# Heads' products of a fused attention and MLP kernel, two groups in a row in the first layer of batches 4 to 7

## The chip, the cores and the metric

The kernel runs on one core of a Trainium2 chip. The metric is the time of one execution on the device in microseconds (us). Engine names are those of the profile: PE (TensorE, matmuls), PEld (its weight loads), ACT (ScalarE), DVE (VectorE), POOL (GpSimd), SP (SyncE, which issues the DMAs).

## The reference

Eight batches, eight heads of 64, 576 tokens; then a layer norm and a two-layer MLP over the 512 columns that the heads make together, with a residual. All inputs are fp32.

```python
# attention, q k v: [8, 8, 576, 64], 32 landmarks = means over 18 tokens each
A = sm(q, k_lm);  Bm = sm(q_lm, k_lm);  C = sm(q_lm, k)      # softmax of scaled products
Z = Bm^T / (norm1(Bm) * norminf(Bm) + 1e-06)
for _ in range(6):
    Z = 2 * Z - Z @ Bm @ Z
x = A @ Z @ C @ v                                             # heads side by side: [8, 576, 512]
# MLP, w_ch1: [512, 2048], w_ch2: [2048, 512]
xn = (x - mean(x)) / sqrt(var(x) + 1e-06) * g_ln
out = x + relu(xn @ w_ch1) @ w_ch2
```

## The kernel before

**The algebra around the change.** The first layer isn't computed from `x`. With `ea` the exponentials of A (already divided by their sums) and `Z C v` small per head (32 landmarks by 64), the product `x @ W1` is taken as `ea^T (Z C v W1)`: per batch, the transposed small matrices `zt` are first multiplied with the (scaled and centred) weights `w1_16`. These are the *heads' products*. They come in four groups `f`, one for each 512 of the 2048 hidden columns. Each group is 8 matmuls with 64 rows and 32 columns of weights (`zt`) and 512 streamed columns, one on each of the eight 64x32 parts of PE's array; they fill two PSUM banks, one for each unit `u` of four heads. ACT or DVE then casts both banks to fp16 into the SBUF tile `m16[f]` (three buffers).

**Chunks.** A batch's hidden values are made in 16 chunks of 128 hidden columns (`chunk(m)`), four to each group: 4 matmuls of 288 columns into `psh`, a PSUM tile of two banks, then one eviction with the ReLU on ACT (or DVE) into `hT`. Chunk `m` reads `m16[m // 4]`. In the kernel before, group 0 is made before chunk 0, and groups 1, 2 and 3 after the chunks 0, 4 and 8: three chunks ahead of their first use.

**Second layer.** `hT` and `w2_16` are multiplied in blocks of 128 tokens, 16 matmuls of 512 columns each, for batches 0 to 3. From batch 4 on (`FAST`) the first four blocks go by `seven_products`, seven products of halves in place of eight, with 256 columns each, whose operands (`w2mix`, and sums within `hT`) POOL and DVE mix beforehand. DVE adds the result, scaled, to `x`, and SP stores it.

**x itself** is made by `rows_of`: matmuls of `ea` with `zcbd` (256 columns, two for each block of tokens), copied out of PSUM by ACT or DVE into `xblk`.

**PSUM.** Eight banks: four single ones (`banks`, L424) that heads' products, rows of `x`, attention's small products and the second layer's sums take in turn, and a ring `ps2` (L421) with two places of two banks each, tag "p2". Attention's scores and sums and every chunk take these places in turn, so a new tile waits until the tile before last has been read out.

**What sets the order of the work.** Every engine runs its instructions in the order in which the program issues them. The program is written by one loop (`run`, L1512) over four streams: attention of the coming batches, first layers, batch 0's rows, second layers. Each stream yields a function that says from when on its next step could run without waiting. The loop goes through the streams in that order and issues the next step of the first one that is ready by its own running estimate of all engines (`Clock`, L83); if none is, of the one that is ready soonest. So a wait in one stream is filled with steps of another, mostly second-layer matmuls, as long as there are any. `help_out` (L1427) issues loads, casts, statistics and mixing on the other engines in between. `sooner` (L518) gives a cast to ACT or DVE, whichever the estimate has free first, and `chunk` does the same for its eviction. Since all instructions go through helpers, nearly all matmuls have line L274 (`MM`) in the profile and nearly all other operations L268; the names of the tiles tell them apart.

The places that the change touches: `First.product_of_heads` (L1138) and `first_layer` (L1174).

Of the kernel before, what the change touches and what calls it, by code (L numbers as in the profile page):

```python
# [10 lines left out]
FP32 = mybir.dt.float32  # L11
# [5 lines left out]
P = 128  # L17
# [3 lines left out]
def kernel(  # L21
# [21 lines left out]
    U = H // 4  # L43
# [10 lines left out]
        name=nc.get_next_instruction_name(), act_func_set_id=6, ins=[], outs=[]))  # L54
# [163 lines left out]
    clock = Clock()  # L218
# [54 lines left out]
    def MM(o, l, r, rb=0, cb=0, start=True, stop=True, skip=False):  # L273
        keep(nc.tensor.matmul(o, l, r, start=start, stop=stop, tile_position=(rb, cb),  # L274
                              skip_group_check=(skip or cb != 0)))
# [75 lines left out]
    for i in range(NV):  # L351
        t = const.tile([P, U, NJ, 2, D + 1], FP16, name=f"natv{i}")
# [9 lines left out]
    for u in range(U):  # L362
        for nm in ("q", "k"):
            t = nat.tile([P, NJ, 2, D], FP16, name="nat", tag="nat")
# [16 lines left out]
    def less(f):  # L381
        return less_[f // 2][:, f % 2, :]
# [35 lines left out]
    mprod = Ring(name="mprod", bufs=3)  # L418
    mhT = ctx.enter_context(tc.tile_pool(name="mhT", bufs=1))

    ps2 = Ring(name="ps2", bufs=2, space=bass.MemoryType.PSUM)  # L421
# [42 lines left out]
    banks = Banks()  # L464
# [53 lines left out]
    def sooner(n, at=0.0):  # L518

        a = max(clock.free["Activation"], at) + 190 + 0.79 * n  # L520
        return scalar.copy if a <= max(clock.free["DVE"], at) + 140 + 1.15 * n else (
            lambda o, i: dve.tensor_copy(out=o, in_=i))
# [607 lines left out]
    class First:  # L1130
# [5 lines left out]
            self.m16 = {}  # L1136

        def product_of_heads(self, f):  # L1138
            self.m16[f] = mprod.tile([P, U, 512], FP16, name="m16", tag="m16")
            psm = [banks.take([P, 512]) for _ in range(U)]  # L1140
            for r in range(2):
                for e in range(2):
                    for u, (w, _) in enumerate(self.units):
                        rows, cb = ds(64 * e, 64), 32 * (2 * (e ^ u) + r)
                        MM(psm[u][ds(cb, 32), :], self.zt[rows, r, w, :],
                           w1_16[rows, 2 * u + r, ts(f, 512)], rb=64 * e, cb=cb, skip=True)
            if f in centered:
                for u in range(U):
                    sooner(512, clock.at(psm[u]))(self.m16[f][:, u, :], psm[u])
                return  # L1150
            n = 2 if (self.b, f) == (0, 0) else 1
            for part in range(n):
                cols = ts(part, 512 // n)
                for u, (_, total) in enumerate(self.units):
                    dve.scalar_tensor_tensor(
                        out=self.m16[f][:, u, cols], in0=less(f)[:, cols], scalar=total,
                        in1=psm[u][:, cols], op0=ALU.mult, op1=ALU.add)
            if self.b == LAST_WHOLE:
                whole.extend((f, c) for c in (0, 2))
# [14 lines left out]
    def first_layer(b):  # L1174
        l1 = First(b)
        if b == 0:
            yield from first_layer0(l1)
            return
        yield lambda: max(banks.next(2), mprod.next("m16"), clock.at(l1.zt))
        l1.product_of_heads(0)  # L1180
        for m in range(MCH):
            yield lambda: max(ps2.next("p2"), clock.at(l1.m16[m // 4], *l1.ea))
            l1.chunk(m)
            if m == 3:
                begun_first[0] = b
            if m % 4 == 0 and m < 12:
                yield lambda: max(banks.next(2), mprod.next("m16"))
                l1.product_of_heads(m // 4 + 1)
        for t in l1.ea:
            aexp.unpin(t)  # L1190
        if b in (0, 1, 2, 4, 6, 7):
            asm.unpin(l1.zt)
# [3 lines left out]
    def first_layer0(l1):  # L1196
        l1.product_of_heads(0)
        scale_w1(5, 1, scalar)
        for m in range(MCH):
            yield lambda: max(ps2.next("p2"), clock.at(l1.m16[m // 4], *l1.ea))  # L1200
            l1.chunk(m)
            chunks0[0] = m + 1
            if m == 0:
                scale_w1(7, 1, scalar)
            if m in (2, 6):
                f = 2 if m == 2 else 3
                for c in range(KCH):
                    yield lambda: max(0.0 if c else banks.next(), clock.at_key(w1_16[:, c, ts(f, 512)]))
                    if c == 0:
                        psf_of[f] = banks.hold([P, 512])  # L1210
                        mine = banks.last
                    MM(psf_of[f][:], lesser[:], w1_16[:, c, ts(f, 512)], start=(c == 0),
                       stop=(c == KCH - 1))
                scalar.copy(less(f), psf_of.pop(f)[:])
                banks.release(mine)
            if m in (1, 5, 9):
                yield lambda: max(banks.next(2), mprod.next("m16"))
                l1.product_of_heads(m // 4 + 1)
# [272 lines left out]
    def first_layers():  # L1491
        for b in range(B):
            yield lambda: 0.0 if b == 0 or (b in ready and current[0] == b - 1
                                            and (b <= LAST_WHOLE or len(centered) == 4)) else NEVER
            yield from first_layer(b)
            first_done.add(b)
            if b >= FAST:
                h_left.extend((b, i, k) for i in range(3) for k in (0, 4))
            if b == 0:
                keep_tail(0)  # L1500
# [109 lines left out]
```

## Time and profile before

| | |
|---|---|
| median of 3 runs | 282.48 us (282.12 to 282.77) |
| the profiled execution | 282.81 us |
| its span, first to last instruction | 281.0 us |
| PE busy | 266.2 us in 3618 matmuls |
| DVE, ACT, POOL busy | 212.3, 161.9, 160.1 us |
| heads' products `bank<-w,zt`, all batches | 256 matmuls in 32 groups |
| chunks `psh<-ea,m` | 512 matmuls, 286 ns each by the profile |
| chunk evictions on ACT, on DVE | 115 of 652 ns, 13 of 750 ns |
| casts into `m16` on ACT, on DVE | 30 of 588 ns, 18 of 679 ns |

Times are of one profiled execution. A row of the timeline has a start, the time from the first start to the last end, engine, line, operation, out<-in by tile names, shape and count, and in brackets the idle time before it and what ended it. A matmul's duration has its pipeline in it: consecutive matmuls overlap, so what a piece costs PE is read from the start of one piece to the start of the next. The page cuts the span into 40 slices of 7.0 us, and gives the busy share of each in tenths.

In the profiled execution the first layers of batches 5, 6 and 7 run from 183.0 to 197.1 us, 205.7 to 219.8 and 239.2 to 253.0, that of batch 4 from 145.8 to 160.5; the attention of batches 5 and 6 is spread from 146.7 to 179 us, that of batch 7 from 220.7 to 235 us, and the second layer fills the rest.

### The profile page before, as it was taken

How to read it: one execution, taken by the hardware profiler on the slowest of the kernel's cores; microseconds unless marked ns; L12 is line 12 of the kernel's file. 1: busy time of each engine (PE TensorE's matmuls, PEld its weight loads, DVE VectorE, ACT ScalarE, POOL GpSimd, SP SyncE). 2: the span in 40 equal slices, each digit the busy share in tenths (PEclk: the TensorE clock that was granted, in tenths of full speed). 3: DMA queues.
4: the chain of work that ended last, by engine and by line, in shares of the span. 5: the costliest groups of instructions: out<-in, count | busy, mean ns of one | idle time of the engine just before them, and what ended most of it. 6: DMA issues, size and time to landing. Idle time of an engine off the chain costs nothing.

```text
span 281.0 us, 8678 instructions
## 1 busy us (share of the span) xinstructions
PE 266.2 (95%) x3618; PEld 165.6 (59%) x3618; DVE 212.3 (76%) x479; ACT 161.9 (58%) x287; POOL 160.1 (57%) x187
## 2 busy tenths in 40 slices
PE   7988999999999999889989999999999999999994
PEld 7744554355444564344555645567877666678883
DVE  3558985999999847888978384697885499748761
ACT  2676954368554887148889754698248733671000
POOL 5368778999999999978999999310000040100000
PEclk9999999999999999999999999999999999999998
DMA  7999999989745579893750101310060005300606
GB/s 244 384 387 388 388 388 392 354 278 266 246 126 160 152 249 304 265 279 95 221 188 2 34 8 45 72 40 0 2 144 9 1 5 118 72 0 2 149 22 167
DMA packets 23375, 46.70 MB, mean 166 GB/s; under 512 B 2212, under 2 KB 2472, under 8 KB 23336
## 3 DMA queue, kind: packets, MB, share of 16 engines
q1 hardware_dynamic: 23176, 46.02, 51.9%
q8 instruction: 28, 0.46, 0.7%
q10 hardware_dynamic: 160, 0.13, 0.2%
q14 instruction: 11, 0.09, 0.1%
HBM read 36.70 MB, written 9.44 MB: 164 GB/s over the span
## 4 chain that ended last, share of the span: by engine, by line
PE 79%; DVE 9%; ACT 5%; issue 3%; DMA 2%; SPq 0%; DVEq 0%; ACTq 0%
PE bank L274 51%; PE psh L274 21%; DMA stg<-in_q_dram 2%; ACT hT L268 2%; DVE xblk L268 2%; PE pscv L274 2%; DVE m L268 2%; DVE xT L268 1%; PE psec L274 1%; PE psd L274 1%; DVE part L268 1%; ACT ec L268 1%; DVE hT L268 1%; ACT lns L268 1%; PE psea L274 1%
## 5 line engine op out<-in xcount | busy, mean ns | idle before, releaser
L274 PE MATMUL bank<-w,hT 128*128 128x512 f16 (+1 forms) x528 | 109.2, 335 | 1.1 <-issue 1.0
L268 ACT ACTIVATE hT<-psh 128x576 f16<-128x576 f32 x115 | 71.0, 652 | 17.4 <-PE psh L274 16.0
L274 PE MATMUL psh<-ea,m 128*128 128x288 f16 x512 | 76.9, 286 | 2.8 <-ACT hT L268 2.1
L274 PEld LDWEIGHTS <-hT 128*128 128x128 f16 x656 | 60.4, 98 | 32.2 <-issue 6.9
L274 PEld LDWEIGHTS <-m 128*128 128x128 f16 x512 | 47.9, 97 | 25.3 <-issue 10.1
L268 DVE SCALAR_TENSOR_TENSOR xblk<-bank,rstd,xblk 128x256 f32<-128x256 f32 (+1 forms) x77 | 39.2, 541 | 18.2 <-PE bank L274 18.2
L268 POOL TENSOR_TENSOR ea<-ea,lns 128x576 f16<-128x576 f16 x14 | 18.1, 1306 | 47.2 <-ACT lns L268 47.0
L268 POOL CAST nat<-stg 128x1152 f16<-128x1152 f32 x28 | 32.6, 1181 | 2.0 <-DMA stg<-in_k_dram 1.1
L268 POOL CAST natv<-stg 64x1152 f16<-64x1152 f32 (+1 forms) x23 | 26.7, 1161 | 8.8 <-DMA stg<-in_v_dram 7.9
L268 ACT COPY xblk<-bank 128x512 f32<-128x512 f32 (+1 forms) x34 | 19.1, 588 | 12.2 <-PE bank L274 12.0
L268 DVE BATCH_NORM_STATS2 six<-xblk 128x6 f32<-128x512 f32 x36 | 24.2, 671 | 0.0
L268 ACT CAST m<-bank 128x512 f16<-128x512 f32 x30 | 17.0, 588 | 9.9 <-PE bank L274 9.9
L268 DVE STREAM_TRANSPOSE xT<-nat 128x576 uint32<-128x576 uint32 x28 | 21.4, 765 | 0.6 <-POOL nat L268 0.6
L268 ACT ACTIVATE lns<-psd 128x576 f32<-128x576 f32 x16 | 10.3, 646 | 17.8 <-PE psd L274 16.7
L268 DVE TENSOR_REDUCE part<-xT 128x32 f16<-128x576 f16 x28 | 20.0, 742 | 0.2
L268 POOL TENSOR_TENSOR asum<-asum 128x256 f32<-128x256 f32 (+1 forms) x28 | 18.0, 644 | 2.2
L268 DVE CAST m<-bank 128x512 f16<-128x512 f32 x18 | 12.2, 679 | 7.3 <-PE bank L274 7.2
L268 POOL TENSOR_TENSOR asum<-nat 128x512 f32<-128x512 f16 x14 | 16.5, 1178 | 1.1
L274 PE MATMUL bank<-w2mix,hT 128*128 128x256 f16 x128 | 16.5, 273 | 0.0
L274 PE MATMUL bank<-w2mix 128*128 128x256 f16 x128 | 16.0, 273 | 0.0
L268 DVE SCALAR_TENSOR_TENSOR st<-st,bank 128x128 f16<-128x128 f16 (+2 forms) x36 | 11.1, 308 | 6.4 <-PE bank L274 6.0
L274 PE MATMUL bank<-zcbd,ea 128*128 128x256 f16 (+1 forms) x80 | 14.4, 275 | 1.0 <-DVE m L268 0.8
(123 smaller groups left out, 341.6 us busy)
## 6 DMA issues: line engine op xcount, KB each, us to landing
stg<-in_q_dram SPq DMA_DIRECT2D x16, 576.0 KB, 5.7
stg<-in_k_dram SPq DMA_DIRECT2D x16, 576.0 KB, 5.4
stg<-in_v_dram SPq DMA_DIRECT2D x16, 576.0 KB, 7.1
out_dram<-xblk SPq DMA_DIRECT2D x70, 128.0 KB, 2.3
wstg<-in_moe_w_ch_dram SPq DMA_DIRECT2D x16, 512.0 KB, 7.1
out_dram<-xblk ACTq DMA_DIRECT2D x2, 64.0 KB, 2.3
out_dram<-xblk SPq DMA_DIRECT2D x2, 64.0 KB, 2.1
g_rows<-in_moe_g_ln_dram SPq DMA_DIRECT2D x1, 2.0 KB
```

The costliest lines, as they stand in the source:

```text
L268: return lambda *args, **kw: keep(getattr(self.engine, op)(*args, **kw))
L274: keep(nc.tensor.matmul(o, l, r, start=start, stop=stop, tile_position=(rb, cb), skip_group_check=(skip or cb != 0)))
```

## The change

For batches 4 to 7, groups 0 and 1 are made together before chunk 0, and groups 2 and 3 together after chunk 4. The first group of each pair takes two of the four single banks as before; the second takes a tile of the ring, one of the two places that the chunks use. All 16 matmuls are issued in a row, then the four casts, first group first. The step waits for two single banks, a place of the ring and two buffers of `m16`. Batches 0 to 3 issue what they did: `product_of_heads` is only split into `products` and `copies`.

```diff
         def product_of_heads(self, f):
+            self.copies(f, self.products(f, [banks.take([P, 512]) for _ in range(U)]))
+
+        def two_products_of_heads(self, f):
+
+            one = self.products(f, [banks.take([P, 512]) for _ in range(U)])
+            t = ps2.tile([P, 2, 512], FP32, name="psm", tag="p2")
+            two = self.products(f + 1, [t[:, u, :] for u in range(U)])
+            self.copies(f, one)
+            self.copies(f + 1, two)
+
+        def products(self, f, psm):
             self.m16[f] = mprod.tile([P, U, 512], FP16, name="m16", tag="m16")
-            psm = [banks.take([P, 512]) for _ in range(U)]
             for r in range(2):
                 for e in range(2):
                     for u, (w, _) in enumerate(self.units):
                         rows, cb = ds(64 * e, 64), 32 * (2 * (e ^ u) + r)
                         MM(psm[u][ds(cb, 32), :], self.zt[rows, r, w, :],
                            w1_16[rows, 2 * u + r, ts(f, 512)], rb=64 * e, cb=cb, skip=True)
+            return psm
+
+        def copies(self, f, psm):
             if f in centered:
                 for u in range(U):
                     sooner(512, clock.at(psm[u]))(self.m16[f][:, u, :], psm[u])
...
-        yield lambda: max(banks.next(2), mprod.next("m16"), clock.at(l1.zt))
-        l1.product_of_heads(0)
+        two = b >= 4
+        if two:
+            yield lambda: max(banks.next(2), ps2.next("p2"), mprod.next("m16", 2), clock.at(l1.zt))
+            l1.two_products_of_heads(0)
+        else:
+            yield lambda: max(banks.next(2), mprod.next("m16"), clock.at(l1.zt))
+            l1.product_of_heads(0)
         for m in range(MCH):
             yield lambda: max(ps2.next("p2"), clock.at(l1.m16[m // 4], *l1.ea))
             l1.chunk(m)
             if m == 3:
                 begun_first[0] = b
-            if m % 4 == 0 and m < 12:
+            if not two and m % 4 == 0 and m < 12:
                 yield lambda: max(banks.next(2), mprod.next("m16"))
                 l1.product_of_heads(m // 4 + 1)
+            if two and m == 4:
+                yield lambda: max(banks.next(2), ps2.next("p2"), mprod.next("m16", 2))
+                l1.two_products_of_heads(2)
```

## The prediction

> **What bounds the kernel now.** I read the page's busy shares and slices first, then the chain of waits, then the PE timeline of the part that the change touches.
>
> ```profile
> PE 266.2 (95%) x3618; PEld 165.6 (59%) x3618; DVE 212.3 (76%) x479; ACT 161.9 (58%) x287; POOL 160.1 (57%) x187
> ...
> PE   7988999999999999889989999999999999999994
> ...
> DVE  3558985999999847888978384697885499748761
> ...
> PEclk9999999999999999999999999999999999999998
> ...
> PE 79%; DVE 9%; ACT 5%; issue 3%; DMA 2%; SPq 0%; DVEq 0%; ACTq 0%
> ```
>
> TensorE (PE) is busy in nine tenths of nearly every slice, at the full granted clock, and 79% of the chain that ends last is PE work. A PE "busy" share alone proves little, so I checked that PE's pieces really follow one another, in the first layer of batch 6:
>
> ```profile
> 207.29 0.65 PE L274 MATMUL psh<-ea,m 128*128 128x288 f16 x4
> 207.88 0.41 PE L274 MATMUL bank<-w,zt 64*32 64x512 f16 x8
> 208.22 1.17 PE L274 MATMUL psh<-ea,m 128*128 128x288 f16 x8
> 209.22 0.38 PE L274 MATMUL bank<-zcbd,ea 128*128 128x256 f16 x2
> 209.44 0.49 PE L274 MATMUL bank<-w,hT 128*128 128x256 f16 x3
> ```
>
> From 146 us (where the batches that the change touches begin) to 277 us PE starts the next piece as soon as the one before has streamed its columns: 8 chunk matmuls take 1.00 us from 208.22 to 209.22, and 8 x 288 columns at the 0.120 us that one matmul needs in longer rows are 0.96. So here a saved PE microsecond is a saved microsecond, and a PE wait costs all of its length. Adding up what exceeds this pattern from 146 to 253 us, I find only some 0.9 us of true waits; from 253 us to the end PE runs 217 matmuls of 256 columns without a gap.
>
> **What a group of heads' products costs PE, and what a pair saves.** A group is the 8 matmuls `bank<-w,zt`, one on each of the eight 64x32 parts of the array. Its price is read from the rows above. Four chunk matmuls before a group last 207.88 - 207.29 = 0.583 us in the exact starts, against 0.490 when chunk or second-layer matmuls follow: 0.10 us to enter the small shape. From the group's start to the next full matmul 0.342 us pass (207.88 to 208.22, and the same in nearly every group). The eight matmuls run side by side, and 512 columns take 0.213 us in the rows of 128x512 matmuls, so 0.13 us is the leaving. The weight loads show the same two stops:
>
> ```profile
> 241.66 0.11 PEld L274 LDWEIGHTS <-zt 64*32 64x32 f16 x8 [0.24 <-issue]
> ...
> 242.00 0.85 PEld L274 LDWEIGHTS <-m 128*128 128x128 f16 x8 [0.23 <-issue]
> ```
>
> The page "TensorEngine Tiling (Array Packing)" of the Trainium skill, section Key Properties, says that a change of tiling mode drains TensorE; it gives no figure, and the rows give it: 0.10 + 0.13 = 0.23 us for in and out.
>
> The changed program puts a second group right behind the first in batches 4 to 7: (0,1) at the batch's start, (2,3) after chunk 4. The second group stays in the same shape. Its cost isn't in the trace; the nearest row is the attention scores, where 32 matmuls of 288 columns lie four deep on eight parts and take 0.607 us: 4 x 0.120 + 0.127, that is full streaming and one way out. So the second group adds its 0.213 us of streaming. The bounds are 0.11 us (only its 8 weight loads; excluded, each part is busy) and 0.342 us (a stop in between). Two single groups cost 2 x 0.445 = 0.89; a pair 0.10 + 0.342 + 0.213 = 0.66. Saved: 0.23 us a pair, two pairs in each of four batches: **8 x 0.23 = 1.85 us**. The order of the built program agrees that this is all on PE: the same 3618 matmuls, and 92 stretches of small shapes in place of 100; the other stretches are as many as before.
>
> **What the change doesn't touch.** SP and POOL issue the same instructions in the same order, so no DMA is moved past another one. On ACT and DVE the same casts and evictions are shared out otherwise (ACT gets 3 chunk evictions of 0.65 us and 5 casts of 0.59 more, DVE 3 of 0.75 and 5 of 0.68 fewer); ACT is 58% busy over the span, and this is hidden behind PE. Without that cover it would be some 4.9 us on ACT.
>
> **The waits that it adds.** The second group stands in one of the two places of tag "p2". The chunks take these places in turn, so the second chunk behind a pair waits until both casts of group f+1 have read it, and these stand behind both casts of group f. The rows:
>
> ```profile
> 241.66 0.41 PE L274 MATMUL bank<-w,zt 64*32 64x512 f16 x8
> ...
> 242.13 0.69 DVE L268 CAST m<-bank 128x512 f16<-128x512 f32 x1 [0.59 <-PE bank L274]
> ...
> 183.80 1.05 ACT L268 CAST m<-bank 128x512 f16<-128x512 f32 x2
> ```
>
> An idle engine starts the first cast 0.47 us after the group's start; two casts on ACT last 1.05, on ACT and DVE side by side 0.69. So the first group's casts are done 1.2 to 1.5 us after the pair's start, the second's 1.8 to 2.1. The pair itself holds PE 0.56 us. What PE does until then is in the built program's order:
> - Batch 4, first pair: 6 second-layer matmuls of 512 columns (1.28 us), chunk 0 (0.48), one more (0.21), chunk 1: the casts are hidden. Batch 6: 9 matmuls of 256 columns (0.98); batch 7: 14 (1.53). Hidden, with 0.1 us to spare or lacking in batch 6.
> - The second pairs stand behind chunk 4. The place that they take was chunk 3's, whose eviction (0.65 us) runs beside chunk 4. Chunk 5 then uses the other place, and 4 to 11 second-layer matmuls stand ahead of chunk 6. Hidden, but for about 0.1 us here and there.
> - **Batch 5, first pair: chunk 0 follows the pair at once.** Attention for batches 5 and 6 now comes after batch 4's first layer, and its waits are filled with batch 3's second layer, 80 matmuls of 512 columns, which is used up exactly here; batch 4's second layer isn't begun yet. Both casts of group 0 stand on ACT: 0.47 + 1.05 + 0.06 = 1.58 us after the pair's start, less the 0.56 of the pair: PE waits **1.0 us**. Nothing else can run: all that stands behind on PE waits in order, evictions and x's rows with it. Bounds: 0.6 (the casts shared out) and 1.5 (ACT also late with the two small activations of 0.5 us ahead of them). Before, this start had two waits of 0.19 us each (at 183.3 and 184.7 us), which go: -0.4.
> - Elsewhere: both score groups of batches 5 and 6 now stand close together, with 1.5 us between them against 1.6 for two exponentials: +0.2. Batch 7's attention now alternates with batch 6's chunks, 0.76 us a turn against 0.65 of an eviction: its waits before (0.4 us) may go. Small waits at the second pairs of batches 5 and 6: +0.1 and +0.2. Together +0.1, between -0.5 and +1.
>
> **The rule that speaks against the change.** The same page, section PSUM Bottleneck, says that tiling speeds up TensorE and not the emptying of PSUM, and that the copy may become the limit. By it every pair would wait for its casts as batch 5's does: 8 x 1.0 - 1.85 = 6 us slower. By the rows, seven of eight pairs have other PE work in between. I take the rows, with one wait.
>
> **End of the kernel.** The last chunk moves from 217 to 206 matmuls of 256 columns ahead of the end, 1.2 us closer. DVE's mixing of batch 7's hidden values (six of 0.68 us, with second-layer sums of 0.48 between them) is needed 94 matmuls or 10.2 us after the last chunk and needs about 6.5: hidden.
>
> **The sum.** -1.85 + 1.0 - 0.4 + 0.1 = -1.15, and for waits that an order on paper doesn't show I add 0.3: **-0.85 us**. On the profiled execution, 282.81 us (span 281.0), that is 281.96; the median of the runs lies 0.33 us below the profiled one, so **281.6 us**. What can be told from no change is 0.2%, 0.56 us: the forecast lies just beyond it.
>
> **Rivals.**
> 1. *The whole gain.* Batch 5's start costs no more than before and the rest is hidden: -1.85 to -2.2, 280.4 to 280.7 us. For it: PE has no waits after 253 us; against it, the order itself.
> 2. *A draw.* The small waits are 0.15 us at most pairs beyond the 1.0: 282.1 to 282.9. Chunk pairs and four matmuls of fill take 1.42 us, against 1.30 for two evictions on ACT; a cast of 0.59 put in between is not covered by that.
> 3. *Slower: the held place stops the chunks.* With one place instead of two, chunk, eviction and chunk run one after another. The place is held 2.1 us from the pair's start, and a late cast then stops PE at each pair. It decides from 0.30 us a pair beyond batch 5's wait (8 x 0.30 = 2.4 us, against 1.85 saved and 0.56 that can't be told); at 0.4 us a pair the time is 283.8 less the 0.4 that goes, some 283.4. For it: DVE is busy to 70 to 90% from 183 to 211 us (slices 27 to 30) and to 90% from 225 to 239, so a cast there can start late; against it: the fill behind seven pairs.
> 4. *The change doesn't do what it says:* the second group drains nonetheless. Then 0.10 of 0.23 us is saved at most, and with batch 5's wait the time is 282.5 to 283. The scores' rows speak against it.
>
> **How the numbers follow.** Forecast 0.5, with 281.0 to 282.3 as its own range; the whole gain 0.13; the draw (with the fourth) 0.17; slower 0.2. Faster by over 0.2% (below 281.9): 0.42 of the forecast's half and all of the first rival, 0.55. Within: 0.07 of the forecast, 0.15 of the draw, and 0.02 of rival 3, 0.24. Slower (above 283.0): 0.21. The range from 280.4 to 283.2 leaves out about 2 in 10.
>
> **What would show it.** Right: 92 stretches of small shapes, pairs of 0.56 us from the first `zt` matmul to the next full one where nothing waits; a PE gap of about 1 us at batch 5's start, ended by ACT's cast into m16; PE full to the end afterwards. Wrong: gaps of 0.3 us and more before the second chunk behind each pair, ended by a cast from `psm`; a second group that starts 0.34 us behind the first; or DVE's iterations of `st` holding PE in the attention of batches 5 to 7.

## The result, and the profile after

The changed kernel is faster: 280.62 us (median of 19 runs, 279.59 to 282.48) against 282.88 us (19 runs, 281.33 to 285.21), a ratio of 0.9924, 95% interval 0.9901 to 0.9947. Forecast were 281.6 us and a gain of 0.85 us; the range (280.4 to 283.2) holds the time, close to its lower end, the direction is right, the gain is larger. Two later measurements of the same kernel gave 0.9956 (0.9920 to 0.9993) and 0.9944 (0.9914 to 0.9975), so a gain of 1.4 to 2.3 us by the differences of the medians.

The page of the changed kernel, the lines that answer to those shown of before (busy shares, PE's slices, the chain):

```profile
PE 264.9 (95%) x3618; PEld 166.1 (59%) x3618; DVE 208.7 (74%) x474; ACT 165.5 (59%) x292; POOL 160.0 (57%) x187
...
PE   7997999999999999879989999999999999999994
...
PE 79%; DVE 10%; ACT 4%; DMA 3%; issue 3%; SPq 0%; DVEq 0%
```

These shares hardly tell the two kernels apart: PE is the limit before and after, with 1.3 us less of busy time, and ACT has taken over some work of DVE. The timeline does. The first pair of batch 4 in the changed kernel (start, length, engine, what, and in brackets the idle time before):

```profile
146.53 0.14 PEld L274 LDWEIGHTS <-zt 64*32 64x32 f16 x16 [0.24 <-issue]
146.54 0.41 PE L274 MATMUL bank<-w,zt 64*32 64x512 f16 x8
146.76 0.40 PE L274 MATMUL psm<-w,zt 64*32 64x512 f16 x8
147.08 0.69 DVE L268 CAST m<-bank 128x512 f16<-128x512 f32 x1 [0.76 <-PE bank L274]
147.09 0.33 PEld L274 LDWEIGHTS <-hT 128*128 128x128 f16 x3 [0.42 <-issue]
```

All 16 weight loads are one piece with one stop ahead of it; the second group starts 0.22 us behind the first, and the next full-size matmul follows at 147.09, 0.56 us behind the pair's start. Both numbers are those of the prediction.

One profiled execution of each kernel doesn't show the gain as the medians do: the spans are 281.0 and 280.3 us. The reason is in the part ahead of the change. Up to the first group of batch 4 both programs issue the same instructions, yet before arrives there at 145.83 us and the changed kernel at 146.54. I therefore cut every profiled execution at that point and measure from the start of batch 4's first products to the start of the last matmul (us):

| kernel | arrives at batch 4 | from there to the last matmul | batch 4 to 5 | 5 to 6 | 6 to 7 | 7 to the end |
|---|---|---|---|---|---|---|
| before | 145.83 | 130.75 | 37.15 | 22.76 | 33.46 | 37.39 |
| before, second profile (e8_before) | 147.61 | 130.75 | 37.14 | 22.75 | 33.46 | 37.39 |
| changed | 146.54 | 129.31 | 34.69 | 24.62 | 32.83 | 37.17 |
| changed, second (e1_again) | 146.21 | 129.32 | 34.69 | 24.62 | 32.84 | 37.18 |
| changed, third (e10_again) | 144.45 | 129.33 | 34.69 | 24.62 | 32.84 | 37.18 |

The columns to the right go from one batch's first products to the next one's. The changed order also moves 12 matmuls for rows of `x` (`bank<-zcbd,ea`) from the first of them into the second, so these two are read together: 0.60 us less. The part that the change touches repeats to 0.02 us, and is **1.44 us** shorter, 0.51% of 282.9 us (ratio 0.9949). The part ahead of it differs by up to 3 us from execution to execution; what the first medians show above 1.44 us I put down to it, which a few profiles can support but not prove (the ratio 0.9949 lies in the two later intervals and just outside the first). All experiments below are read by this stretch first.

### The profile page after: what moved, and what is told of

Its sections match the earlier page's. It is cut to its first block, busy times and chain, and to the rows that moved or that the text cites. A ratio compares the mean times of both kernels' runs of the same rounds, so it can differ in the third digit from the quotient of the medians.

```text
span 280.3 us, 8676 instructions
## 1 busy us (share of the span) xinstructions
PE 264.9 (95%) x3618; PEld 166.1 (59%) x3618; DVE 208.7 (74%) x474; ACT 165.5 (59%) x292; POOL 160.0 (57%) x187
## 4 chain that ended last, share of the span: by engine, by line
PE 79%; DVE 10%; ACT 4%; DMA 3%; issue 3%; SPq 0%; DVEq 0%
PE bank L274 51%; PE psh L274 20%; DVE xblk L268 2%; DMA stg<-in_q_dram 2%; ACT hT L268 2%; PE pscv L274 2%; DVE m L268 2%; PE psec L274 1%; PE psd L274 1%; DVE xT L268 1%; PE psea L274 1%; DVE part L268 1%; DVE hT L268 1%; DMA out_dram<-xblk 1%; ACT lns L268 1%
## 5 line engine op out<-in xcount | busy, mean ns | idle before, releaser
L274 PE MATMUL bank<-w,hT 128*128 128x512 f16 (+1 forms) x528 | 107.9, 335 | 1.3 <-issue 1.3
L268 ACT ACTIVATE hT<-psh 128x576 f16<-128x576 f32 x118 | 73.0, 652 | 14.9 <-PE psh L274 13.4
L274 PE MATMUL psh<-ea,m 128*128 128x288 f16 x512 | 78.0, 286 | 3.6 <-ACT hT L268 2.1
L268 ACT COPY xblk<-bank 128x512 f32<-128x512 f32 (+1 forms) x32 | 18.2, 590 | 11.8 <-PE bank L274 11.1
L268 ACT CAST m<-bank 128x512 f16<-128x512 f32 x24 | 13.2, 588 | 11.0 <-PE bank L274 10.9
L274 PE MATMUL bank<-w2mix 128*128 128x256 f16 x128 | 16.6, 273 | 0.0
L274 PE MATMUL bank<-w2mix,hT 128*128 128x256 f16 x128 | 15.6, 273 | 0.0
L268 DVE STREAM_TRANSPOSE ecT<-ec 128x288 uint32<-128x288 uint32 x14 | 6.4, 466 | 11.3 <-ACT ec L268 10.9
```

The lines of the kernel that those rows point to most:

```text
L268: return lambda *args, **kw: keep(getattr(self.engine, op)(*args, **kw))
```

## The experiments

**The same kernels again (e1_again, e10_again, e8_before).** No edit.

> The changed kernel itself once more, for a second profile and for the ratio on the chip of the other runs. The trace of the first profile loses 0.70 us against the kernel before in instructions that both have alike (up to 146 us), and gains 1.44 us behind them; the runs gain 2.2 us. Theory (the first part differs from execution to execution, the gain of the part behind it is steady): from the first products of batch 4 to the last matmul 1.3 to 1.6 us less than before again, the part ahead of it different by some tenths. Rival (the gain differs too): a stretch that is 2 us or more shorter.

> The kernel before once more, one look. Theory (the part from batch 4 on repeats, the part ahead of it doesn't): 130.7 to 130.8 us from batch 4's first products to the last matmul, with some tenths of difference ahead of it. Rival: that stretch differs by 0.3 us or more from execution to execution.

> The changed kernel a third time, beside e9_halves. Theory: from batch 4's first products to the last matmul 129.3 us, 1.44 us below the kernel before, so a ratio of 0.9949 over many executions. Rival (part of the first measurement's 2.2 us is a real gain outside this stretch): a ratio of 0.993 or below again.

Measured: the table above. Medians 280.83 us against 282.21 (e1_again) and 281.08 against 282.81 (e10_again). The stretch is steady, as both theories had it; the ratio that the rival of e10_again named, 0.993 or below, did not come (0.9944), though it lies in the interval. What follows: the stretch is a measure that is good to some hundredths of a us, the ratio of a dozen runs one that is good to 0.3%, some 0.9 us; the gain in the stretch is 1.44 us.

**Is it the switch of shapes? (e2_stop)** One small full-size matmul between the two groups; its result is overwritten by the second group, and it isn't told to the planner, so the order stays.

```diff
             t = ps2.tile([P, 2, 512], FP32, name="psm", tag="p2")
+            tc.keep_in_program_order(nc.tensor.matmul(
+                t[:, 0, 0:64], zeros[:, 0:P], zeros[:, 0:64], start=True, stop=True,
+                tile_position=(0, 0), skip_group_check=True))
             two = self.products(f + 1, [t[:, u, :] for u in range(U)])
```

> One matmul of 64 columns in the full shape between the two groups of each pair; all else, and the whole order, as in the changed kernel. Theory (what is saved is the leaving and entering of the small shape): each pair gets 0.13 + 0.03 + 0.10 = 0.25 us longer, at batch 5's first pair hidden by the wait for the casts: 7 x 0.25 = 1.8 us above the changed kernel, the second group some 0.47 us behind the first. Rival (the second group stops PE anyway, and the gain is the planner's other order): at most 0.03 us a pair, 0.2 us in all.

Measured: median 281.57 us (ratio 0.9991, 0.9959 to 1.0023); 130.65 us in the stretch, 1.34 us above the changed kernel, almost all that it had gained. The timeline of e2_stop, the same place:

```profile
145.99 0.41 PE L274 MATMUL bank<-w,zt 64*32 64x512 f16 x8
...
146.33 0.10 PEld L1145 LDWEIGHTS <-zeros 128*128 128x128 f16 x1 [0.23 <-issue]
146.34 0.20 PE L1145 MATMUL psm<-zeros 128*128 128x64 f16 x1
146.47 0.11 PEld L274 LDWEIGHTS <-zt 64*32 64x32 f16 x8
146.47 0.41 PE L274 MATMUL psm<-w,zt 64*32 64x512 f16 x8
```

The second group starts 0.48 us behind the first in place of 0.22: 0.26 us a pair, 0.25 expected. It shows in batches 4 (0.64 us for two pairs), 6 (0.36) and 7 (0.33), and not at all in batch 5, where PE waits behind both pairs anyway. In batches 6 and 7 two waits for casts, 0.14 and 0.17 us, which the changed kernel has behind a pair, are gone here, so each shows one of them less than two stops. The theory holds; of the 1.8 us expected 0.5 don't show, since I had counted only one of batch 5's pairs as hidden, and not these two waits. The rival, at most 0.2 us, falls.

**Does the held place cost anything by itself? (e7_place)** The kernel before, its groups at their old points, with groups 1 and 3 of batches 4 to 7 put into a tile of the chunks' ring.

```diff
         def product_of_heads(self, f):
+            if self.b >= 4 and f % 2:
+                t = ps2.tile([P, 2, 512], FP32, name="psm", tag="p2")
+                self.copies(f, self.products(f, [t[:, u, :] for u in range(U)]))
+                return
             self.copies(f, self.products(f, [banks.take([P, 512]) for _ in range(U)]))
...
-        two = b >= 4
+        two = False
```

(and the step's wait asks for `ps2.next("p2")` there in place of two banks.)

> The kernel before, with the groups 1 and 3 of batches 4 to 7 in one of the chunks' two places and not in two single banks, one group at a time at their old points. It has the held place without the saved switches. Theory (the held place costs little where second-layer work stands beside it): from batch 4's first products to the last matmul 130.75 us as before, up to 0.5 more. Rival (the held place stops the chunks, 0.3 us a group or more): 2.4 us more or worse.

Measured: 130.81 us, 0.06 above before; median 282.56 us, ratio 0.9999 (0.9964 to 1.0034). By the columns of the table this is +0.11, +0.05, -0.27 and +0.17: the planner's order has moved a little too. In sum the place costs next to nothing while second-layer work stands beside it. Rival 3 of the prediction, 0.3 us a group, falls.

**Batch 5's wait: other work in between (e3_late_mix).** In the changed kernel, two of the seven products, which read nothing mixed, no longer wait for the mixing.

```diff
     def seven_products(b):
-        while b not in h_mixed:
...
-                mix_ahead()
-        t1, t2, t3, t4, s1, s2 = [t[:] for t in w2_mix]
...
+        yield lambda: clock.at_key(hTs[b][:, MCH - 1, 0:P])
         yield banks.next
         a = bank()
...
         yield from product(e, h12, w21)
+        while b not in h_mixed:
...
+                mix_ahead()
+        t1, t2, t3, t4, s1, s2 = [t[:] for t in w2_mix]
         yield from finished(b)
```

> The changed kernel, with the two of a batch's seven products that read nothing mixed (from batch 4 on) issued before the mixing is waited for. In the program's order 9 second-layer matmuls then stand between batch 5's first pair and its chunk 0. Theory (PE waits 1.0 us there for lack of other work): that wait falls to 0.1 us or less, 0.9 us below the changed kernel, some 3 us (1.1%) below the kernel before. Rival (the wait only moves, to the products that then come without mixed operands or to the rows of x): no more than 0.3 us gained, and a new wait of 0.5 us or more within 10 us behind the pair.

Measured: median 282.34 us (ratio 1.0013, 0.9985 to 1.0041), 130.34 us in the stretch: 1.03 us *above* the changed kernel. The wait at batch 5's start is gone (the nine matmuls stand there), but the second pair, 8.6 us later, shows three new ones. The timeline of e3_late_mix:

```profile
187.78 0.58 ACT L268 COPY xblk<-bank 128x512 f32<-128x512 f32 x1 [0.51 <-PE bank L274]
...
188.42 0.41 PE L274 MATMUL bank<-w,zt 64*32 64x512 f16 x7 [0.36 <-ACT xblk L268]
...
188.98 0.66 PE L274 MATMUL psh<-ea,m 128*128 128x288 f16 x4
...
189.31 1.29 DVE L268 TENSOR_TENSOR w2mix<-w2mix,hT 128x1024 f16<-128x1024 f16 x2
...
190.06 0.33 PEld L274 LDWEIGHTS <-w2mix 128*128 128x128 f16 x4 [0.73 <-DVE w2mix L268]
```

The products' bank is still being copied out as a row of `x`, and after the next chunk PE reaches a mixed operand that DVE makes only now. The batch 5 to 6 column is 24.94 us, 0.3 above the changed kernel, and the 6 to 7 column 33.72, 0.9 above, since batch 7's attention has also moved. The rival holds in substance: the wait moved, and the new order cost more. The longest new wait of PE is 0.59 us by the starts of its matmuls, 10.4 us behind the first pair, where the rival had named 0.5 us within 10.

**Batch 5's wait: shorter casts, same order (e9_halves).** Only for batch 5's group 0: four casts of 256 columns on ACT in place of two of 512, first halves first, and the planner told of the two whole ones.

```diff
+                if (self.b, f) == (5, 0):
+                    for part in range(2):
+                        cols = ts(part, 256)
+                        for u in range(U):
+                            done = nc.scalar.copy(self.m16[f][:, u, cols], psm[u][:, cols])
+                            tc.keep_in_program_order(done)
+                    for u in range(U):
+                        clock.note(Whole(done.ins.engine, self.m16[f][:, u, :], psm[u]))
+                    return
                 for u in range(U):
                     sooner(512, clock.at(psm[u]))(self.m16[f][:, u, :], psm[u])
```

> The changed kernel in its own order, with the two casts of group 0 of batch 5 cut into four of 256 columns, the halves that chunks 0 and 1 read first. Theory (PE waits at batch 5's start for two whole casts one behind the other on ACT): chunk 0 can start after two half casts, 0.47 + 0.27 + 0.38 = 1.12 us behind the pair's start in place of 1.54, so PE's wait there falls from 1.0 to 0.6 us, and from batch 4's first products to the last matmul 128.9 us in place of 129.3. Rival (chunk 0 also waits for something else there, the place, the exponentials or DVE): no change, 129.2 to 129.4 us.

The changed kernel at this place, and then e9_halves (timelines; the bracket is what PE or its weight load waited for):

```profile
181.23 0.41 PE L274 MATMUL bank<-w,zt 64*32 64x512 f16 x8
181.46 0.40 PE L274 MATMUL psm<-w,zt 64*32 64x512 f16 x8
181.70 1.07 ACT L268 CAST m<-bank 128x512 f16<-128x512 f32 x2 [0.76 <-PE bank L274]
...
182.34 0.10 PEld L274 LDWEIGHTS <-m 128*128 128x128 f16 x1 [0.97 <-ACT m L268]
...
182.83 0.54 PE L274 MATMUL psh<-ea,m 128*128 128x288 f16 x3 [0.19 <-ACT m L268]
...
183.30 0.95 PE L274 MATMUL bank<-zcbd,ea 128*64 128x256 f16 x6
```

```profile
181.37 0.82 PE L274 MATMUL psh<-ea,m 128*128 128x288 f16 x4 [0.28 <-ACT m L1173]
182.11 0.95 PE L274 MATMUL bank<-zcbd,ea 128*64 128x256 f16 x6
183.24 0.65 PE L274 MATMUL psh<-ea,m 128*128 128x288 f16 x4 [0.17 <-ACT hT L268]
```

Measured: from the pair's start to the end of chunk 0 in the changed kernel 2.07 us (181.23 to 183.30), where 1.15 would do: 0.56 for the pair, 0.49 for the chunk and 0.10 for the entry into the small shape of the rows of `x` (128x64) that follow. The wait is **0.93 us** by the starts of the matmuls, 0.56 ahead of the chunk's first and 0.37 ahead of its second, and the brackets name ACT's casts. With halves it is 1.65 us (180.47 to 182.11), a wait of 0.50: it falls by 0.43, where 0.4 was expected. But the rows of `x` behind it now take 1.13 us to the next chunk, not 0.81, and wait 0.2 us more before the next but one: 129.44 us in the stretch, 0.13 above the changed kernel; median 281.15 us, ratio 0.9943 (0.9914 to 0.9971), no different. The cause of the wait was named rightly, and removing it gives nothing, because ACT and DVE have casts, evictions and copies of `x` to do one after another here and PE has little else: the bracket of the second chunk already names an eviction. My expectation of 128.9 us and the rival's 129.2 to 129.4 both fail; the first failed by the waits that come next.

**Where the order comes from (e4_from5, e5_7pairs).** Pairs in batches 5 to 7 alone, and pairs in 5 to 7 with one pair (2,3) in batch 4.

```diff
-        two = b >= 4
+        two = b >= 5
```

> Pairs in batches 5, 6 and 7 alone; batch 4's products one by one as before, so the order is that of the kernel before up to batch 5's first layer, where 7 second-layer matmuls of 256 columns follow the pair. Theory (0.23 us a pair, and a wait at batch 5 only where the fill is used up): 6 x 0.23 = 1.4 us, and no wait of 1 us at batch 5's start, so as good as the changed kernel within 0.4 us: 1.2 to 1.8 us below the kernel before. Rival (batch 4's pairs, with their other order of attention, bring the gain beyond 1.85 us): 0.9 us or more above the changed kernel.

```diff
         two = b >= 4
-        if two:
+        if two and b != 4:
...
-            if not two and m % 4 == 0 and m < 12:
+            if (not two and m % 4 == 0 and m < 12) or (b == 4 and m == 0):
```

> As the changed kernel, but batch 4 starts with single groups 0 and 1 and has one pair (2,3) after chunk 4: seven pairs. In the program's order the attention of batches 5 and 6 then begins within batch 4's first layer, as in the kernel before, and 5 second-layer matmuls of 256 columns and rows of x follow batch 5's first pair. Theory (0.23 us a pair; the 1.0 us wait comes from batch 4's first pair, which moves attention behind the first layer): from batch 4's first products to the last matmul 7 x 0.23 = 1.6 us less than before, and no wait of 0.5 us or more at batch 5's start: 129.1 us or less, as e4_from5 or 0.2 us below. Rival (any change of the order costs about as much as it brings): 129.5 us or more.

Measured: e4_from5 129.18 us in the stretch, median 280.63 us, ratio 0.9954 (0.9917 to 0.9990); e5_7pairs 129.95 us, median 281.24 us, ratio 0.9950 (0.9921 to 0.9978). With six pairs and the old order up to batch 5 there is no wait at batch 5's start (pair, 0.56 us, then 7 matmuls), and the stretch is as short as with eight: batch 4's two pairs save 0.46 us and the order that they bring costs 0.6, the difference of the two stretches. That is the theory of e4. With seven pairs batch 5's start is also free of a long wait (22.06 us for the 5 to 6 column, e4 22.01), but the 6 to 7 column is 33.71 us in place of 32.84: there batch 7's attention stands behind batch 6's first layer, as in the kernel before. There PE waits for DVE's iterations, in e5_7pairs:

```profile
224.98 0.24 PE L274 MATMUL bank<-st 32*32 32x64 f16 x8 [0.23 <-DVE st L268]
...
227.87 0.24 PE L274 MATMUL bank<-st 32*32 32x64 f16 x8 [0.28 <-DVE st L268]
```

while in the changed kernel a chunk stands between two iterations and hides DVE's part:

```profile
217.75 0.66 PE L274 MATMUL psh<-ea,m 128*128 128x288 f16 x4
218.35 0.24 PE L274 MATMUL bank<-st 32*32 32x64 f16 x8
218.52 0.66 PE L274 MATMUL psh<-ea,m 128*128 128x288 f16 x4
219.11 0.24 PE L274 MATMUL bank<-st 32*32 32x64 f16 x8
```

So the expectation of e5 fails, and its rival holds: what the planner does with a small shift, 0.9 us here, is as large as four pairs. The 33.71 us are also 0.25 above the kernel before, which has no pair there, so the order of e5_7pairs costs more than that of before too.

**Pairs where PE isn't the limit (e6_batch3).** `two = b == 3`.

> Pairs in batch 3 alone, whose first layer stands where the second layer has little left to fill with: in the kernel before its chunks wait some 3 us for evictions. Theory (a pair saves PE time only where PE is the limit): the 0.46 us of the two pairs don't show; from batch 3's first products to the last matmul (147.8 us in the kernel before) between 0.2 us less and 0.5 us more. Rival (the saving is there wherever the pairs stand): 0.4 us less or better.

Measured: 149.95 us from batch 3's first products to the last matmul against 147.80, 2.15 us *more* (expected 0.5 at most); median 286.04 us, ratio 1.0111 (1.0063 to 1.0158). The saving doesn't show, as the theory had it, but neither its range nor the rival's holds the time. The timeline of e6_batch3:

```profile
138.83 0.38 PE L274 MATMUL bank<-part,spread 128*128 128x256 f16 x2 [1.24 <-DVE xblk L268]
...
139.86 0.72 PE L274 MATMUL bank<-zeros 128*128 128x256 f16 x5
...
140.51 0.41 PE L274 MATMUL bank<-w,zt 64*32 64x512 f16 x8
...
142.91 0.59 ACT L268 CAST m<-psm 128x512 f16<-128x512 f32 x1 [0.53 <-DVE m L268]
...
143.55 1.14 PE L274 MATMUL psh<-ea,m 128*128 128x288 f16 x8 [1.39 <-ACT m L268]
```

PE waits for DVE to empty a bank, and the planner fills with matmuls of zeros: no second-layer matmul stands between 136.2 us and batch 4's start. Behind the second pair the second chunk then waits 1.39 us for the last cast out of `psm`: here the held place does stop PE, as rival 3 of the prediction describes it. By the starts of the matmuls no wait of the kernel before in batch 3's first layer is longer than 0.52 us. The chunks' waits for evictions are no longer than before (1.8 us in all, 2.3 before). How the 2.15 us are shared between the held place and the moved attention (one group of scores more now stands ahead of batch 4), this run doesn't separate.

## Why the prediction was right, and where its sizes were off

- *PE bounds the part; a saved PE microsecond counts.* Right: e2_stop puts the cost of the switch back, with 0.03 us of streaming at each pair, in the same order, and 1.34 of the 1.44 us come back. The waits of before were more than the text says: by the starts of all matmuls from 146 to 253 us they come to some 1.6 us, not 0.9.
- *0.23 us a pair, 1.85 us in all.* Right: the pair takes 0.56 us, and the stop costs 0.26 us with its own 0.03 of streaming. The rows of before give 0.216 and 0.122 us for a matmul of 512 and 288 columns, from start to start, not 0.213 and 0.120; this changes nothing here, since the second group adds 0.215. The bound for a stop in between, 0.342 us, leaves out the entry: with it and its streaming the second group of e2_stop adds 0.48.
- *The casts after the pair are hidden at seven of eight.* Right for the most part. The second pair of batch 5 waits 0.3 us (an eviction on DVE) where 0.1 was put down, and that of batch 6 nothing where 0.2 was. The last cast out of `psm` does hold the second chunk behind a pair twice, by 0.14 us at batch 6's first pair, which the text has on the edge, and by 0.17 us at batch 7's second, in the changed kernel's timeline:

```profile
246.14 0.58 ACT L268 CAST m<-psm 128x512 f16<-128x512 f32 x1 [0.69 <-DVE m L268]
...
246.77 0.90 PE L274 MATMUL psh<-ea,m 128*128 128x288 f16 x6
```

  That is what rival 3 describes, at two pairs of eight and at half its size. Its own sum leaves out batch 5's wait: with that 1.0 us in it, it would decide from some 0.2 us a pair, not 0.30, and 0.4 us a pair would be 284.4 us, not 283.4.
- *Batch 5's first pair waits 1.0 us for ACT's casts.* Right in place, cause and size: 0.93 us. What the trace of before could not show is that this wait can't be taken away for profit (e3_late_mix, e9_halves): it is one form of a shortage of PE work beside ACT's and DVE's.
- *Two waits of before go there, -0.4.* Too much: 0.10 us of the second "wait" was the entry into the small shape, which the same text prices on its own; -0.28.
- *The rest of the sum.* This is the term that was mis-sized: "+0.1" for waits elsewhere and "0.3 for waits that an order on paper doesn't show", together +0.4 us. Measured, it is -1.44 + 1.85 - 0.93 + 0.28 = **-0.24 us**. By batches it is some -0.32 in 4 and 5, -0.16 in 6 and +0.23 in 7, where the wait of 0.17 us above stands. The scores' +0.2 is there (0.16: the second group of `psec`, with its landmark products, holds PE 0.88 us and not 0.72). But the waits of before around attention, which I let off at "may go", went: the second scores (`psea`) hold PE 0.20 us less in batches 5 and 6 and 0.14 less in batch 7, and a wait of 0.23 us ahead of the sums `psd`, at 171.9 us of before, has no like there in the changed kernel. These are readings of the two profiles; no run takes them apart. e5_7pairs shows only that the place of batch 7's attention is worth up to 0.9 us.
- *From 282.81 us to the median.* The sum of 0.85 us was to be seen in the profiled execution; that one lost 0.70 us ahead of the change. The stretch gives 1.44, the medians of three measurements 1.4 to 2.3.
- *Luck.* The median of 280.62 us falls where the first rival, the whole gain, had put it (280.4 to 280.7), and not at 281.6. That rival's reason is not what happened: batch 5's start does cost its 0.93 us. That the time is still in the range owes something to the 0.8 us that the first medians show above the stretch.
- The rule about PSUM's emptying (every pair waits for its casts, 6 us slower) was rightly weighed against the rows for batches 4, 6 and 7, where the waits are 0.17 us at most. In batch 3, without second-layer work, the second pair waits for its casts as that rule has it (1.39 us, e6_batch3).

No kernel here beats the changed one by more than 0.13 us: e4_from5 is that much shorter in the stretch, which its median (280.63 us) can't show.

## What to carry to other kernels

A short stretch of small-shape matmuls costs PE its entry and its leaving, 0.23 us here beside 0.21 of streaming; grouping such stretches saved this at each pair, as long as other PE work covered the longer queue of casts behind them. Where a loop decides the order, its answer to the change can be worth as much as the change: read the new order for the places where the fill runs out, and don't add a lump for the unknown on one side only. And a kernel whose first half differs from execution to execution is compared by the stretch that the edit touches, cut at a common instruction.

## What the runs showed of the hardware that was not expected

The spread between executions of the same program has one main place. Set against e4_from5, matmul by matmul, the other profiles fall behind in jumps ahead of matmuls 1503, 1631 and 1759, which stand 128 apart, by 0 to 3.1 us each, and these start at about 115, 119 and 124 us; the page counts 28 transfers of 0.46 MB together on an instruction queue for 3618 matmuls with as many weight loads, which is one transfer of 16 KB for each 128 or so. PE waits there for nothing that the profile shows ("issue"), while the 16 DMA engines are busy with the loads for later batches: 91 to 100% from 110 to 115 and from 120 to 125 us, 66 to 78% between. The transfers' own records in the traces fit: in all 23 of these waits of 0.15 us and more, over the twelve profiles, PE goes on 1.15 to 1.61 us after a transfer of that queue has ended, and where the transfer had ended more than 1.61 us before the matmul's turn, there is no wait. In the second profile of before (e8_before; the windows view, whose columns are the stretch, its length, busy time of PE, PEld, DVE, ACT and POOL, granted clock, DMA share and GB/s; and the list of waits):

```profile
120.00:125.00 5.00, 2.67 (x32) 1.14 (x29) 4.86 (x13) 2.49 (x4) 4.68 (x7) 1.00 0.97 335
125.00:130.00 5.00, 5.00 (x48) 2.23 (x46) 2.37 (x4) 2.66 (x5) 2.94 (x3) 0.66 0.37 109
```

```profile
PE bank L274 <- issue: 2.3, 1, 2.3
```

The wait of 2.3 us is followed by a stretch with 0.66 of the clock, in which a matmul of 512 columns takes 0.21 us longer. The wait alone doesn't decide that: e2_stop waits 3.1 us at the same place and keeps the full clock behind it:

```profile
125.00:130.00 5.00, 5.00 (x62) 2.25 (x60) 3.51 (x8) 3.39 (x7) 2.93 (x4) 1.00 0.29 76
```

What sets the clock there stays open. That instructions which arrive late behind the loads cause the jumps fits the spacing, the queue and the transfers' times; no experiment here moved them, so it is argued, not shown.
